# Turning the last columns of K and Q by eight 128-column transposes in place of eight 32-column matmuls

## The chip, the cores and the metric

The kernel runs on one core of one Trainium2 chip. The metric is the device time of one execution in microseconds (us); several executions are timed and their median is taken. The profile names the engines PE (TensorE matmuls), PEld (the weight loads of TensorE), DVE (VectorE), ACT (ScalarE), POOL (GpSimd) and SP (SyncE, which only issues transfers).

## What is computed

A gated linear attention with a complex decay, followed by a mixture of experts over the tokens that it gives.

```python
def _attn_ref(q, k, v, a_re, a_im):            # B 4, H 8, S 768, D 48
    ...
    for t in range(S):
        ar, ai = (a_re_n[:, :, t, :, None], a_im_n[:, :, t, :, None])
        new_re = ar * S_re - ai * S_im
        new_im = ar * S_im + ai * S_re
        kv = np.einsum('bhd,bhe->bhde', k[:, :, t], v[:, :, t])
        S_re, S_im = (new_re + kv, new_im)
        y[:, :, t] = np.einsum('bhd,bhde->bhe', q[:, :, t], S_re)

def _moe_ref(x, w_skip, w_gate, w1, w2):       # 3072 tokens of 384, 8 experts of 1024
    ...
    for e in range(E):
        h = np.maximum(xc[mask] @ w1[e], 0.0)
        y[mask] = gate_w[mask, None] * (h @ w2[e])
    out[do_compute] = xc + y
```

## The kernel before, in words

The 768 steps are cut into six chunks of 128, and two chunks make a group, so there are three groups (0, 1 and 2; group 1 is the middle one). In each group a chain on DVE (`chain`, lines 429 and 438) multiplies the decays up, one step after the other; on the 128 partitions lie two directions (sides), two chunks and the 32 pairs of batch and head. `gate` (lines 272 to 379, ACT and DVE) makes the decays for eight steps at a time, and `consume` takes the finished products W of eight steps: it makes `ws` (L498, ACT), sums it on PE (`sw`, L512), inverts it (L520 to L528), and makes the scaled factors `nw` (L503) and `iw` (L531). Eight steps are one piece; a group has eight pieces, and pieces 8 to 15 belong to group 1.

K and Q come out with the steps along the free axis and the pairs along partitions, while the units (below) want the 96 numbers of a step along partitions. So they are turned on PE:

- Groups 0 and 2: `trans` turns every step with a transpose of 128 columns (L659, tile `tp`), four steps to a PSUM tile, and ACT copies the tile out in two copies of 96x256 (L666).
- Group 1 is kept in DRAM (`keep`, L559, POOL's queue) and read back and turned later (`turn`, L598, tile `tu`), apart from its first two units: for these (`NEAR` = 2) the first steps are read back early (`ahead`, L611) and turned by `turn_ahead` (L622, tile `ta`, eight tiles), and the last 24 steps on each side (`ENDS` = 3 pieces: 13, 14 and 15) are turned at once by `straight` from `nw` and `iw`, without a way through DRAM. This is the function that is changed.

`straight` is called six times, once for `nw` and once for `iw` of each of the three pieces. A call makes one PSUM tile `ts` with eight matmuls (L638), one for each step. The step's 128x96 numbers are the weights and the moving operand is a choice of 32 columns of the identity (`some`: for each side the 16 pairs of the two units wanted). Then two ACT copies of 96x128 (L644) bring it to the two tiles `qkT` of the units.

A unit is one batch of one chunk (`unit_at`, `unit`): `pa` is K times Q (L732, 16 matmul records in two tiles), DVE masks it to `at` (L755), PE makes `py` (L802, L805), the state `ps` (L781, L782, L791) and the rows `px` (L817). The first unit of group 1 waits for the copies of `straight`. `wfinal` (L672 to L679, tile `tpe`) turns the end of a group's chain to `E`, from which `make_F` (L688 to L696) starts the next chunk.

`ts`, `ta`, `tp`, `tu` and `tpe` share one PSUM pool, `ps_tp`, with two buffers.

The order of the program is written by a small planner (`Order`): every generator yields how long its step takes on DVE and when it is next due, and `order.pe(cost)` and `order.act(elements, operations)` keep the estimated times at which PE and ACT are free. `straight` is charged with `pe(1400)` and `act(256, 2)` in `trans`. The result `t` of `trans` says when the turned tile is there, and for the last piece of the group the units become due after it. The framework then schedules the program by a timeline of its own (`schedule_with_timeline_sim`), with `issue_after` pinning some instructions.

After the attention come the last two chunks, the routing of the tokens and eight experts (L1229 to L1263, on PE).

Of the kernel before, what the change touches and what calls it, by code (L numbers as in the profile page):

```python
# [9 lines left out]
F32 = mybir.dt.float32  # L10
# [9 lines left out]
B, H, S, D = 4, 8, 768, 48  # L20
DM = H * D
BH = B * H
C = 128
HC = 64
NCH = S // C
NG = NCH // 2
LP = 8
# [17 lines left out]
NEAR, ENDS = 2, 3 * LP  # L45
# [71 lines left out]
class Kern:  # L117
# [513 lines left out]

    def straight(self, i, src, first, jb):

        nc, n = self.nc, NEAR * H
        some = self.ident.rearrange("p (s c n) -> p s c n", s=2, c=2)[:, :, 0, 0:n]
        tp = self.ps_tp.tile([96, LP, 2, n], F32, name=f"ts_{i}_{first}", tag="tp")
        for j in range(LP):
            nc.tensor.matmul(tp[:, j], src[:, j], some, start=True, stop=True)  # L638
        for (c, b), t in self.near.items():
            if first:  # L640
                o = t[:, :, 0:4:3, HC - jb - LP:HC - jb][:, :, :, ::-1]
            else:
                o = t[:, :, 1:3, jb:jb + LP][:, :, ::-1]
            nc.scalar.copy(o, tp[:, :, :, b * H:b * H + H].rearrange("p j s h -> p h s j"))  # L644

    def trans(self, i, src, ql, qr, jb, qk, cost, ss=range(LP // 4)):
        nc = self.nc
        if qk is None:
            t = self.order.t + cost
            if jb >= HC - ENDS:  # L650
                self.straight(i, src, qr > ql, jb)
                t = self.order.act(LP * 2 * NEAR * H, NEAR, self.order.pe(1400, t))
            return t
        t = self.order.pe(475 * len(ss), self.order.t + cost)
        t = self.order.act(512 * len(ss), 2 * len(ss), t)
        for s in ss:
            tp = self.ps_tp.tile([96, 4, 2, 2, BH], F32, name=f"tp_{i}_{s}_{ql}", tag="tp")
            for jj in range(4):
                nc.tensor.transpose(tp[:, jj], src[:, s * 4 + jj], self.ident)  # L659
            jt = jb + s * 4  # L660
            for cc in range(2):
                if qr > ql:
                    o = qk[cc][:, :, 0:4:3, HC - jt - 4:HC - jt][:, :, :, ::-1]
                else:
                    o = qk[cc][:, :, 1:3, jt:jt + 4][:, :, ::-1]
                nc.scalar.copy(o, tp[:, :, :, cc].rearrange("p j s b -> p b s j"))  # L666
        return t
# [816 lines left out]
```

## Time and profile before

| what | value |
|---|---|
| median of 3 runs | 498.83 us (498.48 to 499.66) |
| the profiled execution | 499.22 us |
| its span, first to last instruction | 497.5 us |
| PE busy | 419.4 us (84%) |
| DVE busy | 401.6 us (81%) |
| ACT busy | 301.6 us (61%) |
| POOL busy | 99.5 us (20%) |
| mean granted TensorE clock | 0.906 |

The profile's times count from the first instruction. A granted clock of 1.00 is 2.4 GHz and 0.50 is 1.2 GHz. Busy time of PE is modelled at its ends, so a PE that is shown as busy throughout can still have short gaps; the waits listed say more. An engine's idle time is named with what ended it ("<-").

### The profile page before, as it was taken

The numbers are of one execution on the slowest core, as the hardware profiler recorded it, in microseconds if no ns is written. First come the engines' busy times: TensorE is split into PE (matmuls) and PEld (weight loads), VectorE is DVE, ScalarE is ACT, GpSimd is POOL, SyncE is SP. The second block draws the span as 40 slices with busy tenths as digits, with TensorE's granted clock in tenths as the row PEclk, the third lists the DMA queues.
The fourth block names the chain that finished last, engine by engine and source line by source line (L and its number), as shares of the span: only waits on it lengthen the run. The fifth ranks groups of instructions, "written<-read, shape, count | busy, mean of one in ns | idle before, by whom it ended". The sixth has DMA issues, their size and how long they took to land. (4 is left out here: it accounts for less than half of the span.)

```text
span 497.5 us, 10005 instructions
## 1 busy us (share of the span) xinstructions
PE 419.4 (84%) x3294; PEld 368.3 (74%) x3294; DVE 401.6 (81%) x1009; ACT 301.6 (61%) x702; POOL 99.5 (20%) x173
## 2 busy tenths in 40 slices
PE   0355654399999679999999999999999999999992
PEld 0133333378787568788788889898989999999992
DVE  4999999999989999999989928889777766866630
ACT  5768688666466687578888661333655654655420
POOL 4011111110211512181000110613210211121011
PEclk9966666589999865899999999999999999999997
DMA  4559956589988787896754139676798666865300
GB/s 96 130 127 187 231 131 175 150 203 230 259 215 209 178 195 188 193 243 173 173 148 125 44 97 262 191 192 193 217 285 274 215 193 231 270 187 175 102 24 27
DMA packets 140544, 88.82 MB, mean 179 GB/s; under 512 B 111707, under 2 KB 133164, under 8 KB 140487
## 3 DMA queue, kind: packets, MB, share of 16 engines
q1 hardware_dynamic: 133591, 71.30, 54.7%
q0 software_dynamic: 6256, 16.63, 12.2%
q8 instruction: 28, 0.46, 0.4%
q10 hardware_dynamic: 640, 0.20, 0.2%
q14 instruction: 29, 0.24, 0.1%
HBM read 63.39 MB, written 26.58 MB: 181 GB/s over the span
## 5 line engine op out<-in xcount | busy, mean ns | idle before, releaser
L429 DVE TENSOR_TENSOR X<-W,ain 128x192 f32<-128x192 f32 x192 | 67.7, 353 | 3.5 <-ACT ain L379 0.2
L1154 DVE TENSOR_TENSOR l<-r,h 128x768 fp32r<-128x768 f32 (+1 forms) x53 | 56.6, 1073 | 12.4 <-ACT h L1153 12.3
L512 PE MATMUL sw<-ws,ident 128*128 128x384 f32 x84 | 44.4, 667 | 20.6 <-ACT ws L498 20.5
L1231 ACT ACTIVATE hh<-ph 128x240 fp32r<-128x240 f32 x64 | 23.8, 374 | 55.3 <-PE ph L1229 53.3
L1153 ACT CAST h<-r 128x768 fp32r<-128x768 f32 (+1 forms) x53 | 49.2, 935 | 7.8 <-DMA r<-in_moe_w_dram 6.9
L659 PE MATMUL tp<-ident,iw 128*96 128x128 f32 x128 | 24.7, 347 | 34.0 <-DVE iw L531 34.0
L438 DVE TENSOR_TENSOR W<-X 128x96 f32<-128x96 f32 x192 | 48.7, 254 | 3.6
L1229 PE MATMUL ph<-xh,l 128*128 128x240 f32 x192 | 51.2, 275 | 0.0
L1229 PE MATMUL ph<-xh,h 128*128 128x240 f32 x192 | 49.9, 275 | 0.1
L1229 PE MATMUL ph<-xl,h 128*128 128x240 f32 x192 | 49.5, 276 | 0.2 <-DVE xl L1183 0.2
L659 PEld LDWEIGHTS tp<-ident,iw 128*96 128x96 f32 x128 | 18.8, 161 | 37.9 <-ACT t L286 20.0
L666 ACT COPY qk<-tp 96x256 f32<-96x256 f32 x128 | 39.7, 368 | 9.8 <-PE tp L659 9.3
L1261 PE MATMUL po<-h,hh 128*120 128x384 f32 x128 | 43.5, 340 | 0.7 <-ACT hh L1231 0.7
L512 PEld LDWEIGHTS sw<-ws,ident 128*128 128x128 f32 x84 | 19.6, 257 | 32.8 <-ACT ws L498 22.5
L1262 PE MATMUL po<-l,hh 128*120 128x384 f32 x128 | 42.9, 336 | 0.0
L1263 PE MATMUL po<-h,hl 128*120 128x384 f32 x128 | 41.1, 342 | 0.0
L802 PE MATMUL py<-at,vt 128*64 128x128 f32 x384 | 40.1, 280 | 0.0
L755 DVE TENSOR_TENSOR at<-pa,mask 128x512 f32<-128x512 f32 x48 | 32.3, 684 | 7.2 <-PE pa L732 5.4
L1232 DVE SCALAR_TENSOR_TENSOR hl<-ph,hh 128x240 fp32r<-128x240 f32 x64 | 25.7, 403 | 13.9 <-ACT hh L1231 13.9
L1229 PEld LDWEIGHTS ph<-xh,l 128*128 128x128 f32 x192 | 36.4, 189 | 0.0
L1267 POOL DMA_INDIRECT out_dram<-og,idx x16 | 19.7, 1228 | 83.2 <-DVE og L1266 46.2
L914 POOL DMA_INDIRECT xs<-xa,sl x24 | 26.9, 1121 | 45.5 <-DVE sl L987 20.2
(259 smaller groups left out, 1096.3 us busy)
## 6 DMA issues: line engine op xcount, KB each, us to landing
r<-in_moe_w_dram SPq DMA_DIRECT2D x24, 512.0 KB
r<-in_moe_w_dram SPq DMA_DIRECT2D x32, 384.0 KB
kn<-kq SPq DMA_DIRECT2D x16, 384.0 KB
kq<-nw POOLq DMA_DIRECT2D x24, 192.0 KB, 3.6
kq<-iw POOLq DMA_DIRECT2D x24, 192.0 KB, 4.2
vt<-in_v_dram SPq DMA_DIRECT2D x24, 192.0 KB
out_dram<-xa SPq DMA_DIRECT2D x24, 192.0 KB
ain<-in_a_im_dram SPq DMA_DIRECT2D x90, 48.0 KB
```

The source lines that it names most:

```text
L429: V.tensor_tensor(X, prev.unsqueeze(1).to_broadcast([128, 2, 2, D]), windows(ain[:, :, j]), ALU.mult)
L438: self.cins = V.tensor_tensor(W[:, j, ::-1], X[:, :, 0], X[:, :, 1], ALU.add).ins
L512: nc.tensor.matmul(sw, self.ident, ws[:, :, c], start=(c == 0), stop=(c == 1))
L659: nc.tensor.transpose(tp[:, jj], src[:, s * 4 + jj], self.ident)
L666: nc.scalar.copy(o, tp[:, :, :, cc].rearrange("p j s b -> p b s j"))
L802: PE.matmul(py[j * 64:j * 64 + 64, hp], vt_[:, 2 * hp + j], at[:, 2 * hp + j], start=True, stop=(c == 0))
L1153: nc.scalar.copy(hi[:, ks], raw)
L1154: nc.vector.tensor_tensor(lo[:, ks], raw, hi[:, ks], ALU.subtract)
L1229: pe = PE.matmul(ph, w[:, k, js], x[:, k], start=(n == 0), stop=(n == len(terms) - 1))
L1261: PE.matmul(po, hh[:, j, sl], w2h[:, j], start=(j == 0), stop=False)
L1262: PE.matmul(po, hh[:, j, sl], w2l[:, j], start=False, stop=False)
L1263: pe = PE.matmul(po, hl[:, j, sl], w2h[:, j], start=False, stop=(j == NF - 1))
```

## The change

`straight` is rewritten after the pattern of `trans`: each step is turned with a transpose in transpose mode of all 128 partitions, four steps to a PSUM tile, so a call now makes two tiles, and each tile is copied out in two copies of 96x64 (of a step's 128 columns the eight heads of one batch, on each of the two sides; the rest of the tile is not read). The planner's charge goes from 1400 to 950 on PE and from two to four operations on ACT. Nothing else is edited.

```diff
     def straight(self, i, src, first, jb):
 
-        nc, n = self.nc, NEAR * H
-        some = self.ident.rearrange("p (s c n) -> p s c n", s=2, c=2)[:, :, 0, 0:n]
-        tp = self.ps_tp.tile([96, LP, 2, n], F32, name=f"ts_{i}_{first}", tag="tp")
-        for j in range(LP):
-            nc.tensor.matmul(tp[:, j], src[:, j], some, start=True, stop=True)
-        for (c, b), t in self.near.items():
-            if first:
-                o = t[:, :, 0:4:3, HC - jb - LP:HC - jb][:, :, :, ::-1]
-            else:
-                o = t[:, :, 1:3, jb:jb + LP][:, :, ::-1]
-            nc.scalar.copy(o, tp[:, :, :, b * H:b * H + H].rearrange("p j s h -> p h s j"))
+        nc = self.nc
+        for s in range(LP // 4):
+            tp = self.ps_tp.tile([96, 4, 2, 2, BH], F32, name=f"ts_{i}_{s}_{first}", tag="tp")
+            for jj in range(4):
+                nc.tensor.transpose(tp[:, jj], src[:, s * 4 + jj], self.ident)
+            jt = jb + s * 4
+            for (c, b), t in self.near.items():
+                if first:
+                    o = t[:, :, 0:4:3, HC - jt - 4:HC - jt][:, :, :, ::-1]
+                else:
+                    o = t[:, :, 1:3, jt:jt + 4][:, :, ::-1]
+                nc.scalar.copy(o, tp[:, :, :, 0, b * H:b * H + H].rearrange("p j s h -> p h s j"))
 
     def trans(self, i, src, ql, qr, jb, qk, cost, ss=range(LP // 4)):
...
                 self.straight(i, src, qr > ql, jb)
-                t = self.order.act(LP * 2 * NEAR * H, NEAR, self.order.pe(1400, t))
+                t = self.order.act(LP * 2 * NEAR * H, 2 * NEAR, self.order.pe(950, t))
```

## Rows read from the trace of the kernel before

**Rows 1.** The page's second part: busy tenths of each engine in 40 equal slices

```profile
PE   0355654399999679999999999999999999999992
DVE  4999999999989999999989928889777766866630
```

**Rows 2.** Line 638, all its matmul records: ns min/median/max, first and last start

```profile
L638 PE MATMUL ts_True<-ident,nw x48: 193/347/348, 166.4 to 191.4; 128*96 128x32 f32 x48
...
L638 PE MATMUL ts_False<-ident,iw x48: 340/348/369, 171.7 to 195.0; 128*96 128x32 f32 x48
```

**Rows 3.** Waits of DVE from 215 to 300 us: total, times, longest

```profile
DVE F L688 <- ACT E L679: 6.4, 1, 6.4
DVE at L755 <- PE pa L732: 4.7, 6, 1.9
```

**Rows 4.** Waits of PE from 203 to 299 us, the longest one

```profile
PE sw L512 <- ACT ws L498: 0.2, 1, 0.2
```

**Rows 5.** Stretches: length, busy PE, PEld, DVE, ACT, POOL, granted clock, DMA

```profile
73.33:75.25 1.92, 1.92 (x9) 1.42 (x7) 1.64 (x6) 1.89 (x6) 0.00 (x0) 0.50 0.44 103
83.09:84.10 1.01, 1.01 (x9) 0.78 (x7) 0.98 (x4) 0.81 (x2) 0.00 (x0) 1.00 0.59 113
...
182.00:195.80 13.80, 12.90 (x78) 12.09 (x78) 13.38 (x35) 12.02 (x34) 3.72 (x6) 0.50 0.70 177
195.80:202.20 6.40, 6.38 (x22) 5.02 (x23) 6.31 (x26) 1.41 (x4) 0.60 (x1) 0.50 0.80 196
202.40:290.00 87.60, 87.23 (x765) 71.83 (x764) 79.71 (x214) 70.00 (x177) 18.79 (x26) 1.00 0.61 150
```

**Rows 6.** Timeline of PE: start, length, line, count; in brackets the idle time before

```profile
73.33 1.92 PE L659 MATMUL tp<-ident,nw 128*96 128x128 f32 x8
...
83.09 1.04 PE L659 MATMUL tp<-ident,nw 128*96 128x128 f32 x8
...
166.37 1.47 PE L638 MATMUL ts_True<-ident,nw 128*96 128x32 f32 x16
...
192.59 2.74 PE L638 MATMUL ts_False<-ident,iw 128*96 128x32 f32 x16 [0.82 <-ACT qkT L644]
...
195.82 3.79 PE L732 MATMUL pa<-qkT 96*128 96x128 f32 x16
199.40 2.77 PE L512 MATMUL sw<-ws,ident 128*128 128x384 f32 x4
...
203.02 1.06 PE L732 MATMUL pa<-qkT 96*128 96x128 f32 x8
```

**Rows 7.** Lines 644 and 666, ACT copies: ns min/median/max, first and last start

```profile
L644 ACT COPY qkT<-ts_False x6: 243/262/264, 174.5 to 195.7; 96x128 f32<-96x128 f32 x6
...
L666 ACT COPY qk<-tp x128: 347/368/392, 23.5 to 297.7; 96x256 f32<-96x256 f32 x128
```

**Rows 8.** Timeline of ACT

```profile
59.41 1.16 ACT L666 COPY qk<-tp 96x256 f32<-96x256 f32 x4
...
187.66 0.53 ACT L289 ACTIVATE t<-sq 128x384 f32<-128x384 f32 x1
...
192.13 0.40 ACT L644 COPY qkT<-ts_True 96x128 f32<-96x128 f32 x2
...
195.10 0.52 ACT L379 ACTIVATE ain<-ain 128x384 f32<-128x384 f32 x1
195.53 0.41 ACT L644 COPY qkT<-ts_False 96x128 f32<-96x128 f32 x2
```

**Rows 9.** Timeline of DVE

```profile
188.51 0.95 DVE L375 TENSOR_TENSOR ain<-ain,t 128x768 f32<-128x768 f32 x1
...
191.49 0.95 DVE L531 TENSOR_TENSOR iw<-inv,W 128x768 f32<-128x768 f32 x1
...
291.00 0.69 DVE L755 TENSOR_TENSOR at<-pa,mask 128x512 f32<-128x512 f32 x1 [1.93 <-PE pa L732]
299.07 0.22 DVE L688 TENSOR_TENSOR F<-E,E 96x64 f32<-96x64 f32 x1 [6.44 <-ACT E L679]
```

## The prediction, made before the change was run

> **What bounds the kernel now.** I read the busy tenths of the engines first [rows 1]. DVE is full almost everywhere up to about 285 us, and from about 100 us PE is nearly full too (but for a dip around 170 us), so neither decides by its share alone. The one slice in which DVE is empty (a 2, at 286 to 298 us) is where the middle group's units end. The six calls that change lie between 166 and 196 us [rows 2], so I then asked who waits in the stretch behind them. DVE has two kinds of waits there: 4.7 us in six waits of the mask `at` on the scores `pa`, and one of 6.4 us for `E` [rows 3]. Both come from PE, directly or by one ACT copy behind it. PE, in turn, waits from 203 to 299 us for nobody longer than 0.2 us [rows 4], and it is shown busy for 87.23 of 87.60 us [rows 5]. So from the first unit of the middle group (its `pa` starts at 195.82 us, [rows 6]) to 299 us the time is set by PE working through its queue: whatever brings that start forward, or lets PE work faster behind it, arrives at 299 us. Before that start DVE is the bound: 13.38 of 13.80 us busy between 182 and 195.8, against 12.90 for PE at half clock and 12.02 for ACT [rows 5]. Nothing of the change touches DVE's own work. No rows are needed for what follows 299 us: the later stages begin with `E` and move with it.
>
> **PE, removed and added.** A call now shows 16 matmul records for eight steps, 48 for three calls [rows 2]; at full clock a call takes 1.47 us, at half clock 2.74 us [rows 6]. The transposes of the other groups are the same operation as the new ones, 128x96 numbers against 128 columns: eight of them, as eight records, take 1.04 us at full clock and 1.92 us at half [rows 5, 6]. So a call loses 0.43 us at full and 0.82 us at half clock. One call (166.37) runs at full clock, the other five at half, or 0.43 + 5 x 0.82 = 4.5 us of PE time in all. Most of this is worth nothing: at 182 to 195.8 us PE is not what is waited for, and the calls of pieces 13 and 14 are over microseconds before anybody reads the tile. What counts is the last call (192.59): its `iw` is finished by DVE at 191.49 + 0.95 = 192.44 us [rows 9], PE starts 0.15 us later, and the first `pa` waits for the copies behind it. Here the saving is at most 0.82 us.
>
> **ACT, removed and added.** Twelve copies of 128 columns go, 24 of 64 columns come. One copy of 128 takes 0.26 us, two in a row 0.41 us, so the second adds 0.15 us; one of 256 takes 0.37 us, four in a row 1.16 us, so each further one adds 0.26 us [rows 7, 8]. From 128 to 256 columns the step grows by 0.11 us; for 64 columns I estimate 0.15 - 0.055 = 0.10 us for a further copy and 0.26 - 0.055 = 0.21 us for the first. Four copies then take 0.21 + 3 x 0.10 = 0.51 us, 0.10 more than now, or 0.6 us over six calls. The upper bound counts each of the two extra copies with a whole 0.26 us: 0.5 us per call, 3.1 us in all. I take 0.10, since rows of copies in a row show that they overlap. The lower bound is nought: the first tile's copies can run while PE turns the second half.
>
> **The end of the last call.** Now its copies begin at 195.53 us, not when PE is done (192.59 + 2.74 = 195.33) but behind `ain` (L379, until 195.62, overlapping the copy's start) [rows 6, 8]. The first unit needs two of the four new copies, the first of each tile. If ACT's order stays as it is, the needed third copy starts 2 x 0.10 us after 195.53 and ends at about 195.94, against 195.79 now (one copy): a loss of 0.15 us. If the schedule, in which the tile is ready earlier, puts the copies ahead of `ain`, the whole 0.82 us is gained. The first unit starts between 0.15 us later and 0.82 us earlier. Between the two I take the earlier end, since the schedule is made afresh with the shorter PE work and ACT is short of work right behind (1.41 of 6.40 us busy, [rows 5]).
>
> **The clock behind it.** From 195.8 to 202.2 us the granted clock is 0.50, from 202.4 us on 1.00 [rows 5]; it rose after PE had been working without a stop, last on the four 384-column `sw` [rows 6]. If the rise stays where it is, PE has 0.82 us more at half speed before it, which is 0.41 us of full-speed work. If it comes forward with the work, the full 0.82 us stays. I take 0.4 us.
>
> **PSUM, queues, planner.** Two buffers serve all turned tiles, and a call takes both in place of one, so its second tile waits for the copies of the call before. For the last call these end at 192.13 + 0.40 = 192.53 us [rows 8], before the second tile would start: nothing. The calls of piece 14 follow the eight `ta` tiles and may wait for a copy; the cover is that their `qkT` is read only at 195.8 us, and without that cover it would be a copy's 0.4 us. No transfer is issued or moved on SP's or POOL's queue, no wait is added there. The planner's charges shift its estimates: PE by -450 ns, ACT by +190 ns (two operations of 95), the due time of the units by -260 ns. That costs no time itself but can change the order of the program from 166 us on; that is a rival.
>
> **Sum.** 497.5 us of span and 1.7 us around it are the profiled 499.2 us; the change makes it 498.8 us. The profiled execution lies 0.4 us over the median of 498.83 us, so the median forecast is 498.83 - 0.4 = 498.4 us. A measurement of this kernel tells a difference from none at about 0.2%, or 1.0 us: the forecast is no change that can be told. By its own bounds it lies between 498.0 and 499.0 us.
>
> **Rival 1, faster: the new order.** The stretch behind is one queue of PE whose order decides what DVE waits for. The wait of 1.93 us at 291.00 and the 6.44 us for `E` at 299.07 [rows 9] arise because PE does other things first. Units that become due 0.26 us earlier in the plan can move a `pa` or the end of the chain forward in the queue. With the 1.93 us wait gone besides the 0.4 us, the time is 496.5 us. For it: PE is never short of work there, so an order with the right thing first is a pure gain. Against it: a planner that reacts to 0.2 us may as well put the wrong thing first.
>
> **Rival 2, slower: ACT falls behind.** Between 182 and 195.8 us ACT is busy 12.02 of 13.80 us [rows 5] and works strictly in order; DVE's `ain` (188.51) needs `t`, which ACT finishes at 187.66 + 0.53 = 188.19 [rows 8, 9], a slack of 0.32 us. The copies of three calls stand ahead of such steps. At 0.5 us extra per call (the upper bound) this is 1.5 us, less the slack 1.2 us, and DVE, the bound there, hands it on: 498.83 + 1.2 = 500.0 us. It decides from about 0.3 us extra per call. Against it: rows of copies overlap.
>
> **Rival 3, slower: the clock rises later.** The sixteen-record calls at 182 to 195.8 us kept PE 12.90 us busy and did not raise the clock [rows 5], so their replacement by lighter work need not lower it either. But if the half clock lasts through the next work of PE, eight transposes cost 1.92 - 1.04 = 0.88 us more and sixteen `pa` 3.79 - 2 x 1.06 = 1.67 us more [rows 6], 2.5 us together, and with the 0.4 us gained 501.0 us. The Trainium skill (TensorE: Matmul & The Clock Gate, Part 4: PE-mode transpose) says that the full clock does not engage for transposes, because they do not count as PE work in the same way. By that rule the calls themselves stay at half clock, and no call would help to raise it; the trace does not settle it, since eight transposes ran once at 0.50 and once at 1.00 [rows 5, 6], each time behind `sw`. The `sw` and `pa` that come before the rise stay real matmuls, which is why I give this little.
>
> That the change does not do what it says (transposes that show as two records each, so that PE saves nothing) would leave 498.8 us and belongs to the same sign as the forecast.
>
> **How the numbers follow.** Forecast (with the case of no saving): 0.42. Rival 1: 0.33, since the order is made anew and PE's queue is where time is lost. Rival 2: 0.15. Rival 3: 0.10. So faster 0.33, same 0.42, slower 0.25. The range reaches down past rival 1 (496.5) by a third of a microsecond and up past rival 2 (500.0) by as much again as its slack and the estimate of the copies leave open, 0.8 us: 496.2 to 500.8 us; rival 3 and the far end of rival 1 stay out. The forecast's own range is 498.0 to 499.0 us.
>
> **What would show it.** Right: calls of eight records at 1.0 to 1.9 us in place of 16; four copies in 0.5 us; the first `pa` of the middle group 0 to 0.8 us earlier; the clock's rise at 202 us or before; `E` at 299 us earlier by as much as the start. Wrong: DVE waiting for ACT between 182 and 196 us (rival 2), a granted clock of 0.50 beyond 203 us (rival 3), or waits of `at` and `E` that shrink or grow by more than the start moved (rival 1 or its mirror image).

## The result, and the profile after

The changed kernel takes 504.11 us (four runs, 503.26 to 505.29); the kernel before, run beside it, 498.92 (498.48 to 499.66). The ratio is 1.0107, with a 95% interval of 1.0091 to 1.0123: slower by 5.2 us and outside the predicted range. The profiled execution took 505.29 us, the longest of the four; its span is 503.5.

The calls themselves came out as costed. All matmul records of line 638 after the change (columns as in [rows 2]):

```profile
L638 PE MATMUL ts_True<-ident,nw x24: 272/421/446, 167.0 to 191.0; 128*96 128x128 f32 x24
L638 PE MATMUL ts_False<-ident,iw x24: 421/421/446, 173.0 to 195.6; 128*96 128x128 f32 x24
```

The 96 records are now 48. The timeline of PE shows a call at full clock, one at half clock, and the last one with the first `pa` behind it (columns as in [rows 6]):

```profile
166.98 1.04 PE L638 MATMUL ts_True<-ident,nw 128*96 128x128 f32 x8
...
184.93 1.91 PE L638 MATMUL ts_True<-ident,nw 128*96 128x128 f32 x8
...
194.06 1.91 PE L638 MATMUL ts_False<-ident,iw 128*96 128x128 f32 x8 [2.65 <-DVE iw L531]
...
196.79 3.42 PE L733 MATMUL pa<-qkT 96*128 96x128 f32 x16
```

And the four copies of the last call on ACT:

```profile
195.98 0.52 ACT L645 COPY qkT<-ts_False 96x64 f32<-96x64 f32 x4
```

A call of 1.47 us became 1.04, one of 2.74 became 1.91; four copies take 0.52 us. These are the durations of the working. The loss is elsewhere. The stretches of [rows 5] after the change (length; busy PE, PEld, DVE, ACT, POOL; granted clock; DMA share, GB/s):

```profile
182.00:195.80 13.80, 9.77 (x47) 7.11 (x44) 13.41 (x35) 11.83 (x38) 3.71 (x6) 0.53 0.75 175
...
200.00:220.20 20.20, 15.52 (x133) 12.10 (x132) 18.96 (x68) 12.05 (x33) 7.89 (x8) 1.00 0.83 200
220.40:223.60 3.20, 3.20 (x9) 1.68 (x8) 1.56 (x5) 1.18 (x4) 1.56 (x2) 0.50 0.52 131
224.00:290.00 66.00, 66.00 (x592) 55.14 (x592) 59.12 (x146) 52.68 (x132) 6.43 (x14) 1.00 0.55 132
```

Up to 195.8 us PE is spared 3.1 us (9.77 busy for 12.90) and DVE stays as full as it was. From 200 to 220.2 us PE is idle for 4.7 of 20.2 us, where the kernel before had no wait over 0.2 us, and behind that it stands at half clock for 3.4 us (220.3 to 223.7). Before, it had full clock from 202.4 us on without a break [rows 5]. The waits of PE from 203 to 299 us say for whom it waited, where [rows 4] had nothing over 0.2 us:

```profile
PE tu L598 <- ACT qkT L600: 2.8, 2, 2.5
PE tp L660 <- ACT ain L328: 1.8, 1, 1.8
```

and DVE, from 215 us on, waits for PE in new places besides those of [rows 3]:

```profile
DVE F L689 <- ACT E L680: 6.9, 1, 6.9
DVE at L756 <- PE pa L733: 2.3, 3, 1.3
DVE ws L523 <- PE tu L598: 1.5, 1, 1.5
...
DVE RX L771 <- PE ps L783: 1.1, 1, 1.1
```

The 2.5 us have a cause that can be read on ACT's timeline:

```profile
218.47 0.48 ACT L833 COPY xa<-px 128x384 f32<-128x384 f32 x1 [2.73 <-DMA xs<-xa,sl]
218.85 0.20 ACT L836 COPY xa<-tok 128x4 f32<-128x4 f32 x1
218.95 0.58 ACT L520 ACTIVATE ws<-sw,col 128x384 f32<-128x384 f32 x1
219.42 1.06 ACT L600 COPY qkT<-tu 96x512 f32<-96x512 f32 x2
```

The rows of the first unit of chunk 2 (`xa`, two buffers, so this one was last used by chunk 0) may be written only when chunk 0's rows have been scattered. Before, this copy stood behind the four `qkT<-tu` copies and waited for nothing:

```profile
215.49 1.89 ACT L600 COPY qkT<-tu 96x512 f32<-96x512 f32 x3
217.74 0.58 ACT L600 COPY qkT<-tu 96x512 f32<-96x512 f32 x1 [0.36 <-PE tu L598]
218.22 0.48 ACT L832 COPY xa<-px 128x384 f32<-128x384 f32 x1
```

Now it stands ahead of them, waits 2.73 us, and the turned tiles of unit (2,2), which PE waits for, are queued behind it. Nobody wrote that order by hand: the framework orders the program by its own timeline. Counted by line and tile in the order of the two traces, without the calls' own records, 389 of 3198 records on PE, 85 of 695 on ACT and 174 of 1014 on DVE have changed places.

**The account.** The stage ends with the copy of the third `E` on ACT (L679 before, L680 after):

```profile
298.65 0.38 ACT L679 COPY E<-tpe 96x256 f32<-96x256 f32 x1
```

```profile
303.34 0.38 ACT L680 COPY E<-tpe 96x256 f32<-96x256 f32 x1
```

PE alone from 205 us to that copy (length, busy PE, granted clock, DMA share, GB/s), first before, then after:

```profile
205.00:298.65 93.65, 93.28 (x834) 1.00 0.58 146
```

```profile
205.00:303.34 98.34, 93.39 (x818) 0.98 0.59 143
```

The length is idle time, plus half of the stretch at half clock, plus the work that was left at 205 us, at full clock. Before: 0.37 + 0 + 93.28. After: 4.95 + 1.70 + 91.69. PE had 1.6 us less left to do (its clock rose at 199.9 instead of 202.3 us, which by itself is worth up to 1.2 us); it lost 4.6 us idle and 1.7 us at half clock: +4.7 us, of the span's +6.0; where the other 1.3 us go, behind the third `E`, was not traced. The profiled runs below are read with this sum.

### The profile page after: what moved, and what is told of

Read it like the earlier page. It is cut to its first block, busy times and chain, and to the rows that moved or that the text cites. A ratio compares the mean times of both kernels' runs of the same rounds, so it can differ in the third digit from the quotient of the medians.

```text
span 503.5 us, 9920 instructions
## 1 busy us (share of the span) xinstructions
PE 418.0 (83%) x3246; PEld 363.8 (72%) x3246; DVE 403.5 (80%) x1009; ACT 302.2 (60%) x714; POOL 99.9 (20%) x173
## 5 line engine op out<-in xcount | busy, mean ns | idle before, releaser
L512 PE MATMUL sw<-ws,ident 128*128 128x384 f32 x84 | 43.6, 655 | 20.9 <-ACT ws L498 20.6
L1230 PEld LDWEIGHTS ph<-xh,h 128*128 128x128 f32 x192 | 35.6, 189 | 0.3 <-issue 0.2
```

The source lines that it names most:

```text
L512: nc.tensor.matmul(sw, self.ident, ws[:, :, c], start=(c == 0), stop=(c == 1))
L1230: pe = PE.matmul(ph, w[:, k, js], x[:, k], start=(n == 0), stop=(n == len(terms) - 1))
```

## The experiments

Theory A: the order alone costs it, by the ACT wait above. Theory B: the calls' new form (transposes, four copies, two PSUM tiles) costs it. Theory C: the order is worse in many places. Theory D came up on the way: PE that runs ahead must wait, and half clock follows. In the expectations of the last five runs A stands for the idle time as the loss, and D for the half clock behind it.

### One wait taken out, one put in, and the calls' copies alone

```diff
 # e1: after; the rows of unit (2,0) are held until unit (2,2) is turned
+            if nx == (2, 2):
+                with self.tc.issue_after(self.tu_ins):
+                    self.held()
...
+        if (c, b) == (2, 0):
+            self.held = store
...
 # e2: before; the tu copies of unit (2,2) queue behind the rows of (2,0)
+                with self.tc.issue_after(self.tok_ins) if (c, b) == (2, 2) else ExitStack():
                     nc.scalar.copy(o[:, :, :, ::-1] if q else o, tp)
 # e3: before; 32-column matmuls, but two tiles and four copies of 96x64 a call
+        for s in range(LP // 4):
+            tp = self.ps_tp.tile([96, 4, 2, n], F32, name=f"ts_{i}_{s}_{first}", tag="tp")
...
```

> The changed kernel, in which ACT makes the copy of the first middle unit's rows (xa from px, with the token column and the store) only behind the four copies of the third unit's turned K and Q (qkT from tu); nothing else is edited. Theory A (the loss is one wait on ACT: the copy to xa stands ahead of the qkT copies and waits for the scatters that still read that buffer): most of the 5.2 us comes back, 499 to 501 us, with no idle time of PE over 1 us before tu and no clock of 0.50 near 220 us. Theory B (the new form of the six calls costs the time itself): 503 to 505 us as before. Theory C (the order is worse in many places, this wait is one of them): 501 to 503 us.

Measured: 504.58 us (500.94 to 508.83, ten runs), ratio 1.0114 (1.0075 to 1.0153). Four runs lie at 500.9 to 501.8 us, five at 505.9 to 508.8, one between them.

> The kernel before, in which the four qkT copies of the third middle unit are held on ACT behind the copy to xa and its token column; the six calls are as in the kernel before. Theory A: the wait for the scatters appears on ACT at about 216 us, PE idles for 2 us and more, and the time is 502 to 505 us. Theory B: within 1 us of the kernel before, since the calls are not touched. Theory C: a part of the loss, 500 to 502 us.

Measured: 506.50 us (505.92 to 507.34), ratio 1.0152 (1.0133 to 1.0171).

> The kernel before with its 32-column matmuls, but two PSUM tiles of four steps to a call and four copies of 96x64 in place of one tile and two copies of 96x128: the copies and buffers of the changed kernel without its transposes. Theory B with the copies or buffers as the cause: 503 to 505 us. Theory B with the transposes as the cause: 498.5 to 499.5 us. Theory A: the copy to xa stands here behind three of the four qkT copies, so the wait holds back one copy alone: 499 to 501 us.

Measured: 499.42 us (496.90 to 501.12), ratio 1.0002 (0.9987 to 1.0018).

None of the three is as clean as its edit looks, for the framework orders each program anew: counted as above, 394 PE records change places in e1 against the kernel after, 567 in e2 and 269 in e3 against the kernel before. So each tests its edit together with a new order. With that said: the copies and the second PSUM tile cost nothing that shows (e3), and an order with the rows' copy ahead of the `tu` copies, with the calls untouched, costs more than the whole change (e2). The wait of ACT is in its trace:

```profile
217.93 0.48 ACT L833 COPY xa<-px 128x384 f32<-128x384 f32 x1 [2.00 <-DMA xs<-xa,sl]
```

PE stands idle at the same place, the clock falls (219.9 to 223.3 us), and the account is 4.95 idle + 1.70 + 93.43. But it is `RX` of DVE that ends this idle time, not the ACT copies: the rest of `tu` and the `pa` of the next unit, which filled the time in the kernel before, stand behind `ps` in the new order.

```profile
219.56 1.32 PE L782 MATMUL ps<-RX,ident 96*96 96x384 f32 x2 [2.39 <-DVE RX L771]
```

```profile
205.00:305.08 100.08, 95.13 (x834) 0.98 0.55 134
```

In e1 the wait is gone, and still the profiled run (501.61 us) ends its stage 1.9 us late, with 2.10 idle + 1.70 + 91.76: the first idle time of the kernel after (1.8 us, until 213.5 us) is still there, and now it is this one that half clock follows, from 214.0 to 217.4:

```profile
PE tp L660 <- DVE nw L503: 1.9, 1, 1.9
...
205.00:300.56 95.56, 93.46 (x828) 0.98 0.60 147
```

In this run 2.8 of the stage's 4.7 us are gone with the wait. The median of the ten runs shows no gain over the kernel after (504.58 for 504.11 us), so theory A is not borne out by it. What the runs of 506 to 509 us do is open: none of them has a profile.

### The calls and the order, crossed

Both programs were built with every instruction but the calls' own pinned, on every engine, to the order of the other one (edges of issue order, no waits added):

```diff
+        for a, b in zip(seq, seq[1:]):
...
+            tc.add_manual_dep(ins[b], ins[a].name, dep, reason="order of another program")
```

The first time they ran, with the kernels before and after beside them, the chip was one on which the kernel before itself takes 514.45 us.

> The transposes and copies of the kernel after, every other instruction on every engine in the order of the kernel before (edges of issue order alone, no waits). Theory A (the loss is the order alone: it lets TensorE idle at 211 to 220 us and fall to half its clock): not slower than the kernel before of the same batch; by the earlier rise of the clock it saw in the kernel after (199.9 for 202.3 us) 0 to 1.6 us faster; on a chip where before takes 498.9, 497.3 to 499. No wait of TensorE over 0.6 us from 205 to 290, no stretch at granted clock .50 there. Theory B (the transposes and the four small copies a call cost it themselves): 4 to 6 us slower than before.

> The 32-column matmuls and two copies a call of the kernel before, every other instruction on every engine in the order of the kernel after. Theory A: 4 to 6 us slower than the kernel before, as the kernel after is: the rows' copy of unit (2,0) waits 2 to 3 us for the scatters of chunk 0, TensorE idles over 2 us in each of two places from 205 to 226, and a stretch at granted clock .50 follows. If the lead that the earlier clock gives matters, up to 1 us slower still. Theory B: within 1 us of the kernel before.

> The kernel after, beside the two runs on the same chip. Theory A: within 1 us of the run with before's operations in this order, 4 to 6 us above before. Theory B: within 1 us of the run with its operations in before's order.

> The kernel before, for its profile on the same chip: TensorE busy for 93 us from 205 us to the third copy of E, under 0.6 us idle in any one place. Both theories the same.

Measured, beside 514.45 us: after in before's order 515.48 (ratio 1.0016, 0.9979 to 1.0053), before in after's order 512.04 (0.9987, 0.9946 to 1.0027), after 510.65 (0.9958, 0.9920 to 0.9996), before 512.16 in its one run. Nothing of the loss shows; the kernel after is even a little faster, so on this chip the crossed pair decides nothing. In the two profiled runs (e11 and e10, spans of 510.4 and 511.0 us) the third `E` of the kernel after still comes 2.4 us later than that of before (303.3 for 300.9 us), and the spans differ by 0.6 us alone, so a later stage makes up for the rest. Where, is not shown; there is slack behind it, as from 345 to 390 us PE is busy for about 40.5 of 45 us in both, where it was busy for 43.6 in the kernel after on the first chip. Before and after, in this order:

```profile
345.00:390.00 45.00, 40.52 (x349) 1.00 0.71 218
```

```profile
345.00:390.00 45.00, 40.49 (x330) 0.96 0.66 207
```

Four earlier runs had fallen on this chip too. In e4 and e5 the rows of unit (2,0) go to a free value buffer; the gate weights of these rows are left out there.

```diff
+        xa = self.vts[2].rearrange("p h k -> p (h k)")[:, 0:XW] if (c, b) == (2, 0) else self.xa[c][:, b]
```

> The kernel after, but the rows of unit (2,0) go to a buffer of their own (the third value buffer, which is given up after unit 7 instead of unit 11), so that their copy on ScalarE no longer waits for the scatters of chunk 0, and the token column is copied in two parts. The framework orders the instructions anew (some 150 lines on TensorE and 220 on ScalarE differ from the kernel after). Theory A (one ScalarE wait and the fall of the clock behind it are the loss): 497.5 to 500.5 us, no wait of that copy for a transfer, TensorE busy for over 9.5 of the 10 us from 216 to 226 and no new stretch at granted clock .50 there. Theory B (the transposes themselves cost it): 503 to 505. Theory C (many orders are worse in many places): anywhere from 499 to 507, with the waits in other places.

> The kernel before with the same buffer of its own for the rows of unit (2,0): the control for the run beside it, as it changes the value loads and the order as well. Theory A: 498 to 500.5 us, since the copy did not wait there anyway; and within 1.5 us of the after kernel with the same edit. Theory B: 4 to 6 us faster than the after kernel with the same edit. Theory C: 499 to 507, in no fixed relation to that one.

> The kernel with the rows of unit (2,0) copied behind the four turns, once more, for its profile: its ten runs lay at about 501.5 and at about 507 us. Theory A: either time has TensorE busy for about 10 of the 10 us from 216 to 226; a run of 507 would have a wait elsewhere that the profiled run of 501.6 did not have, and theory A would not say where. Theory C: a run of 507 shows a wait of over 2 us of TensorE in another place, before or after, with a stretch at granted clock .50 behind it.

> The kernel after, once more, for its profile. Both theories 503 to 505.5 us. Theory A: the copy of the rows of unit (2,0) waits 2 to 3 us for the scatters of chunk 0, TensorE is busy for 7 to 8 of the 10 us from 216 to 226. Theory C: the time is lost in another place than in the first profile.

Measured, beside 514.32 us: 519.18 (e4, ratio 1.0092, 1.0051 to 1.0133), 521.41 (e5, 1.0160, 1.0080 to 1.0241), 514.69 (e6) and 509.88 (e7). e4 and e5 order the program anew as well, and both are slower than the kernels that they come from: that is as theory C has it, but on this chip it says nothing of the 5 us. The crossed pair was run again, on a chip where before takes 498.83 us.

> The transposes and copies of the kernel after, every other instruction in the order of the kernel before, once more. On a chip where before takes about 499 us: theory A (the order costs it) 498 to 500.5 us, the third copy of E within 1.5 us of that of before, TensorE idle for under 1 us in all from 205 to 240; theory B (the calls cost it) 503 to 505. A third possibility, seen in the first run of this kernel: the transposition of E waits 2.2 us for the four copies of the last call, which costs up to 1.2 us at 196 and no more. On a chip where before takes 514: 513 to 517 whichever holds.

> The matmuls and copies of the kernel before, every other instruction in the order of the kernel after, once more. On a chip where before takes about 499 us: theory A 503 to 506 us, the third copy of E 4 to 7 us later than in before, TensorE idle for 4 to 5 us from 205 to 226; theory B 498 to 500. On a chip where before takes 514: 510 to 516 whichever holds.

Measured: the calls of after in before's order 502.33 us (500.76 to 504.57), ratio 1.0070 (1.0044 to 1.0096). The calls of before in after's order 503.94 us (502.60 to 504.47), ratio 1.0096 (1.0079 to 1.0113). In both traces every record of PE, ACT, DVE and POOL but the calls' own stands in the order of the other program. So the order alone costs 5.1 us, the whole of the loss; but the calls alone cost 3.5, which neither theory forecast, and together they cost 5.2, not 8.6. Theory B falls as the cause of the 5 us, since e13 loses them without the new calls, and theory A falls as the whole of it, since e12 loses 3.5 us without that ACT wait.

e13 loses mostly by idle time, with no half clock behind it. Its waits of PE from 205 us on are those of the kernel after, the wait of ACT for the scatters is there, and its account is 4.66 idle + 0 + 94.59. Of the 5.6 us by which its third `E` is late, 4.3 are idle time and 1.3 are work still left at 205 us: its first `pa` starts at 197.94 for 195.82 us, and its clock rises at 204.7 for 202.3 us.

```profile
221.09 0.48 ACT L832 COPY xa<-px 128x384 f32<-128x384 f32 x1 [2.29 <-DMA xs<-xa,sl]
```

```profile
PE tu L598 <- ACT qkT L600: 2.3, 2, 2.1
PE tp L659 <- DVE nw L503: 1.9, 1, 1.9
```

```profile
205.00:304.25 99.25, 94.59 (x840) 1.00 0.59 142
```

e12 is the run to learn from. In before's order its clock already rises at 194.2 us, so `pa`, `sw` and `tp` run at full clock, and the router's matmul starts at 204.3 instead of 207.1 us: PE is 2.8 us ahead. Then:

```profile
203.90 0.43 PE L803 MATMUL py<-at,vt 128*64 128x128 f32 x2
...
207.57 1.67 PE L660 MATMUL tp<-ident,iw 128*96 128x128 f32 x8 [2.91 <-ACT st L785]
209.03 2.69 PE L792 MATMUL ps<-vt,kn 128*96 128x48 f32 x16
```

```profile
206.58 0.61 ACT L285 ACTIVATE sq<-sq,col 128x384 f32<-128x384 f32 x1 [3.45 <-DVE sq L284]
207.11 0.46 ACT L785 COPY st<-ps 96x384 f32<-96x384 f32 x1
```

What PE needs next lies behind the chain on DVE, which is where it was in the kernel before:

```profile
206.49 0.62 ACT L285 ACTIVATE sq<-sq,col 128x384 f32<-128x384 f32 x1 [2.02 <-DVE sq L284]
```

There `tp<-iw` started at 207.47 us, here it starts at 207.57: the whole lead is gone. And behind the idle time stands half clock, in the stretch below and a little beyond it (207.8 to 214.7 us):

```profile
207.90:214.60 6.70, 6.70 (x51) 0.50 0.51 127
...
205.00:301.75 96.75, 93.99 (x815) 0.96 0.57 141
```

The account is 2.76 idle + 3.45 + 90.54. Against before, PE had 2.7 us less to do, gave 2.4 back as idle time and lost 3.45 by the clock: +3.1 us, which is also what its span shows. That is theory D, read from one trace. The seven runs of this program on this one chip lie apart (three at 500.8 to 500.9 us, four at 502.3 to 504.6); the profiled one, 502.33, is of the second group.

### Is PE the bound, and is it the idle time or the clock?

22 or 9 matmuls that nobody reads stand behind the router's matmuls, where e12 idles:

```diff
+            for k in range(22):                       # 9 in e16 and e18
+                PE.matmul(pz[:, 256:384], self.ident, self.mask, start=True, stop=True)
```

> The kernel before in its own order with the same 22 matmuls in the same place. Theory D and theory A alike: TensorE has no idle time between 205 us and the third copy of E there, so the copy comes 2.5 to 3.5 us later and the kernel takes 501 to 503 us beside a before of about 499. If it stays within 0.5 us of before, TensorE is not what sets the end of this stage, and both theories fall.

Measured: 502.67 us (501.63 to 503.93), ratio 1.0074 (1.0051 to 1.0097). This is more than was expected: each of the 22 is two records, so they take 5.2 us, not 2.9. In the profiled run all of it arrives, the third `E` comes 5.2 us later:

```profile
205.00:303.85 98.85, 98.48 (x881) 1.00 0.56 138
```

So in the kernel before PE's queue does set the end of this stage, microsecond for microsecond; of the median's time 3.6 us of it are left. As this program is pinned too, to its own order, the run also shows that the pins by themselves add nothing to this stage: PE is busy for 93.28 us plus the 5.2, and idle for 0.37 us as before.

> The transposes of after in before's order, with 22 matmuls of 128 columns (about 2.9 us at full clock) behind the router's matmuls of chunks 0 and 1, where TensorE idled for 2.9 us; their result lies beside the router's and nobody reads it. Theory D (TensorE that runs ahead must wait for VectorE's gate chain, and the half clock behind that wait is the loss): no stretch at .50 from 205 to 220, the third copy of E within 1 us of that of before, 498 to 500.5 us beside a before of about 499, that is 2 to 4 us less than without the added work. Theory A (the idle time is the loss): no gain from useless work, 502 to 505.

Measured: 502.74 us (501.21 to 503.87), ratio 1.0075 (1.0052 to 1.0099). That lies in the range of theory A and not in that of D. The idle time and the half clock behind 205 us are gone (97.08 of 97.45 us busy), but the added work is over 2 us longer than the gap that it fills, and VectorE's router waits 3.6 us for it; and in this execution the clock fell earlier, from 197.5 to 200.9 us. So it doesn't decide; hence nine of them, twice, the first time with the control beside it:

> The transposes of after in before's order, with 9 added matmuls (2.0 us) where TensorE idled 2.9 us. Theory D (the half clock behind the idle time is the loss): no stretch at .50 of more than 3.5 us between 203 and 225, the third copy of E within 1.3 us of that of before, 498.5 to 501 us beside a before of about 499, and 1.5 to 3 us below the run without added matmuls. Theory A (the idle time is the loss): within 0.7 us of the run without them, or above it.

> The same kernel without added matmuls, the control: 500.7 to 504.6 us as in its last run, TensorE idle for 2 to 3 us at about 205 us and at granted clock .50 for 3.4 to 6.9 us behind it. Theory D: where a run has no such stretch behind it, it is not over 500.5 us. Theory A: all runs alike.

> The transposes of after in before's order with 9 added matmuls (2.0 us), once more. Beside a before of about 499 us: theory D (the half clock behind the idle time is the loss) 499 to 501 us, 1.3 to 3 us below the 502.33 us without added matmuls, and in the profiled run no stretch of 6.9 us at granted clock .50 behind 203 us; theory A (the idle time is the loss) 502 to 504.5 us. Beside a before of about 514 us: no verdict.

Measured: e16 514.14 (ratio 1.0031, 0.9983 to 1.0078) and e17 515.59 (1.0074, 1.0036 to 1.0111), beside a before of 513.52, on another chip of the slower kind; e18 501.45 (498.80 to 502.49), ratio 1.0041 (1.0022 to 1.0060), beside 498.85. Both times the short filling lies 0.3 to 0.4% under the kernel without it (e16 beside e17 on one chip, e18 beside e12 on two), which is the way of theory D, but the intervals overlap, and e18's 501.45 us lies in the range of neither. In e18's profiled run the clock was up for good only from 203.1 us, so that PE had no lead and no idle time and simply paid for the added work; in e16's PE idled 3.0 us at another place, until 222.7 us, without a named cause, and half clock followed from 224.0 to 227.5. The pair leans to theory D and doesn't settle it.

What e17's profile adds: it is the same program as e12, with the clock in another phase. Its half clock lies from 197.9 to 201.3 us, ahead of the critical stretch, PE idles 1.2 us in place of 2.9, and behind that the clock stays up:

```profile
205.00:216.00 11.00, 9.59 (x91) 1.00 0.81 192
```

Its `at` of unit (2,1) starts 0.6 us later than in the kernel before, where that of e12 starts 3.1 us later. The order and the operations are the same; where the half clock lies differs, and with it the lead, the idle time and most of the loss up to that point. It is no test of the half clock alone: e17 ran on another chip, its idle time is shorter too, and its third `E` (301.49 us) comes only 0.2 us ahead of that of e12, as PE waits there for another 1.6 us without a named cause.

## Why the prediction was wrong

**What held.** PE is the bound from 205 to 299 us in the kernel before (e15), and DVE is as full ahead of that as the prediction had it. The durations of the new calls are those of the rows of `tp` (1.04 and 1.91 us). Four copies took 0.52 us against an estimate of 0.51. Rival 2 fell: from 160 to 215 us DVE waits 0.9 us in all (0.8 before), 0.5 of it for ACT's `t` at `ain` (0.3 before), and from 182 to 195.8 us it is as busy as it was (13.41 us for 13.38). Rival 3 fell as it was put: the clock rose at 199.9 us in the profile after and at 194.2 in e12, earlier than before. The Trainium skill (TensorE: Matmul & The Clock Gate, Part 4: PE-mode transpose) says that the full clock does not engage for transposes. These traces do not agree: a call of eight ran at clock 1.00 in 1.04 us, and in e12 PE did nothing but transposes (`ta`, `ts`) from 179 us until its clock rose at 194.2.

**The step that failed** is the sum's silent term: that the order of the program stays, and with it the row that PE waits for nobody over 0.2 us [rows 4]. I costed every instruction in its old place and took the saving of the last call (0.4 us) as all that passes on. The first `pa` came no earlier at all (196.79 for 195.82 us, of which 0.6 us were there before the first call), because DVE's `iw` of the last call was itself 1.5 us later in the new order (0.6 of it that same shift). I named a new order as rival 1, but only as a gain: "PE is never short of work there, so an order with the right thing first is a pure gain". That sentence is the error. PE is not short of work in the kernel before because it is late: half clock until 202.3 us keeps it just behind DVE's chain. Give it 2 to 3 us and it waits, as in e12, or the order puts a wait in front of it, as in the kernel after. The mirror image of rival 1, which the prediction names twice ("may as well put the wrong thing first") and gives no price, is what happened: from 205 us to the third `E` PE idles for 4.95 us in place of 0.37 and loses 1.7 us at half clock, and `E` comes 4.7 us later. That the order alone is enough for such a loss is measured (e13, 5.1 us); that the two waits of PE carry it is read from the traces.

**The second failed step** is the clock. I had it fall or rise with the kind of work. In these runs it fell behind idle time: 2.5 us in the profile after, 2.4 in e2, 1.9 in e1, 2.9 in e12. It didn't fall behind every one: in e13 PE idled 1.9 and 2.1 us and the clock stayed up. I costed no half clock after 203 us except as rival 3, 2.5 us; the runs where it fell show 1.7 to 3.45.

**Smaller misses.** The term of PSUM, put at nothing, left out `tpe`, which shares the two buffers and stands ahead of the first `pa`: it waited 0.36 us for the copies of the last call in the profile after, and 1.50 us in e12, where `pa` therefore starts at 196.22 us though the call before it ended 0.9 us earlier than in the kernel before.

```profile
195.96 0.42 PE L678 MATMUL tpe<-ident,e 128*96 128x128 f32 x2 [1.50 <-ACT qkT L645]
```

The last call's wait in the kernel before was ended by the copies of the call ahead of it (until 192.53 us), as its row in [rows 6] says, and not by `iw` (192.44 us); that changes the sum by 0.09 us at most. And what follows `E` does not simply move with it: in the kernel after `E` was 4.7 us later and the span 6.0 us longer, in e15 5.2 and 4.2.

**The planner's charges**, which I gave as the way in which the order would change, do nothing: as built with the old charges the program after keeps its order to the last instruction, and so does the program before with the new ones. It is the framework's own timeline that reorders, by the operations alone.

**What stays open.** How the 3.5 us of e12 divide between idle time and clock rests on the account and on two traces of one program, not on a kernel that differs in the clock alone. Which of the reordered places costs the rest of the kernel after beyond the two waits, and what the slower runs of e1 do, was not found. The clean form of e1, the program pinned to after's order with that one copy moved, was not run, so the price of the ACT wait by itself is not shown. A third buffer for `xa`, which would remove the wait, was not tried. On the chips where the kernel before takes 499 us, no version was faster beyond the noise.

## What to carry to other kernels

A row that says "this engine never waits" describes one order and one timing: before a saving on the engine that is the bound is counted, look at what it would run into if it came a few microseconds earlier, and price that wait. When the order is made by a scheduler, a change of operations can change the whole order behind it, and so can an edit that is meant as a test of one wait; pin the order if one thing alone is to be tested. For the critical stretch, list which instruction could move ahead of which on each in-order engine, and what it waits for. And measure on more than one chip: here the same pair was 1.0% slower on one and 0.4% faster on another.

## What the runs showed of the hardware

- TensorE's granted clock fell to 0.50 behind idle times as short as 1.9 us (e1: idle until 213.97, half clock from 214.0 to 217.4 us) and as long as 2.9 us (e12: 207.8 to 214.7). The length of the idle time alone did not decide: behind 1.8 us until 213.5 us in the kernel after, 1.9 us until 213.8 us in e10, and 1.9 and 2.1 us until 216.7 and 222.7 us in e13 it did not fall. A `ps` of two records takes 1.49 us at half clock and 0.81 at full.
- One program met the clock in different phases in three executions on three chips: its rise near 200 us lay at 194.2 us in e12; in e17 and e8 it rose at 194.5 and 193.0 and fell again, until 201.3 and 203.2 us.
- Chips differ by 3%: the kernel before took 498.8 to 499.1 us in the batches on four chips and 513.5 to 514.5 us on two others, where PE's waits behind 200 us include 2 to 8 us for which the profile shows no cause, against at most 0.2 us on the four.
